# Attention and two bilinear layers on one core: v windows of 96 rows instead of 128, and a new order of the opening

## The chip, the cores and the metric

The kernel runs on one core of a Trainium2 chip. The metric is the device time of one execution in microseconds (us). The engines are named as in the profile: PE (TensorE matmuls; PEld its weight loads), DVE (VectorE), ACT (ScalarE), POOL (GpSimd) and SP (SyncE, which here issues every DMA).

## What is computed

The reference, cut to what matters (batch 2, 8 heads, 768 positions, head size 64; 1536 tokens of width 512):

```python
k_sum = k.reshape(B, H, nb, 32, D).max(axis=3)
v_sum = v.reshape(B, H, nb, 32, D).mean(axis=3)
scores_l = where(abs(i - j) < 16, scale * q @ k.T, -1e9)
scores_s = scale * q @ k_sum.T + log(32)
a = softmax(concat([scores_l, scores_s]))
x = a @ concat([v, v_sum])              # 1536 x 512 after the heads are put side by side
h = x @ w_in                            # d_ff 2048
x = (h * tanh(softplus(h))) @ w_out     # the first layer ("mish")
out = ((x @ w_a) * (x @ w_b)) @ w_out2  # the second, d_ff 1536
```

## The kernel before

**Attention.** Queries are cut into units of 64 (`U`). A unit sees 96 keys (`WK` = 64 + 2 x 16) and the 24 block sums, 120 columns in all (`SW`). Four units are a group g; there are six groups, three of each batch, and four pairs of heads p in each. For a pair, `batch_s` (L567, L571) makes the scores on PE, DVE adds the mask and finds the row's extreme with a custom instruction (L588, one per unit and head side; below "score pass"), ACT takes the exponential (L594), DVE sums, inverts and multiplies (L597, L599, L601, the last below "weight product"). `batch_o` transposes the weights on PE (L626), copies them out of PSUM (L377 on ACT or L378 on DVE), and multiplies by v (L638; for group 0 the sums' part apart, L651). The result x is kept as a rounded high part (CAST, L377/L378) and a low part (L668).

**Where v lies.** `load_windows` brings for each of the four units its window of v with the unit's first row in partition 0. Rows 96 to 119 of the same tile take the block means of v, which `prep_v` makes on PE (L492), `keep_v` copies out and `spread_v` copies by a DMA from SBUF to SBUF (`attn<-attn`). The block maxima of k are DVE reductions (L462). The windows of before are 128 partitions high, so that the spread must follow them.

**The layers.** `step1` does the first layer on the tokens that are ready, four slices of 128 columns of d_ff: L897 is x @ w_in, L927 the mish on ACT, L930 its low part, L944 the product with w_out. Weights come as 64-bit numbers; `convert` makes 32-bit ones of them (ACT L688, DVE L693 and L696) and `split` the high (ACT L377) and low (DVE L708) parts. After the attention follow the other slices of the first layer (L1076, L1121) and the second one (L1076, L1229), both on PE without a pause.

**What sets the order.** Every step is handed to a planner (`Plan`) with a due time and a cost on each engine that may do it. `emit` runs the plan through a list schedule (ready steps, earliest key first) and writes each engine's instructions in that order; on the chip each engine then keeps the order and waits by semaphores. Due times hang on `T0` (start of the first layer), `bt`/`out_t` (scores and output of a group) and `pace`. DMA durations, the extra key for a switch of ACT's function table (`TABLE_PENALTY`) or of PE's tile shape (`SHAPE_PENALTY`) are constants of the planner. Where PE would stand idle before `fill_end`, a matmul on a zero tile is put in, whose result nobody reads (`fill`, L434); eight of them also open the program:

```python
if pick is None and e == "PE" and ham_end > 3.5 and t < self.fill_end:
    ...
    pick = (t, e, "fill", fb[-1])
...
pl.fill, pl.fill_end = fill, T0 + -7.99
```

Of the kernel before, what the change touches and what calls it, by code (L numbers as in the profile page):

```python
# [34 lines left out]
class Plan:  # L35
# [8 lines left out]
    SAME, PE_SHAPE = 0.02, 0.095  # L44
    SHAPE_PENALTY = 1.6
    PINNED = -50.0
    DMA_LEAD, DMA_TAIL, DMA_RAMP = 0.62, 2.18, 8.0
    BACKLOG, DMA_SLACK, DMA_RING = 4.0, 0.5, 8
    TABLE, TABLE_PENALTY = 1.3, 5.37
    WARM, PAGE, PE_LEAD, FETCH, FETCH_BUSY = 0.34, 256, 64, (6.4, 2.6), 46.0  # L50
# [38 lines left out]
    def emit(self):  # L89
# [18 lines left out]
        ready = {e: [] for e in engines}  # L108
        free_at = {e: 0.0 for e in engines}
        bank_free, where, held = {b: 0.0 for b in range(8)}, {}, set()  # L110
# [12 lines left out]
        while done < n:  # L123
# [94 lines left out]
            if delay:  # L218
                dma_free = max(dma_free, end + self.DMA_LEAD) + delay * (1.35 if 2.0 < dma_free < self.DMA_RAMP else 1.0)
                end = dma_free + self.DMA_TAIL  # L220
                landed.append(end)
# [19 lines left out]
def attention_mish_moe_bilinear_moe(  # L241
# [23 lines left out]
    U = 64  # L265
# [7 lines left out]
    NEG = -1.0e9  # L273
    T0 = 20.47
    BITS64 = w_in.dtype != F32
# [484 lines left out]
    size = lambda b: GT * len(gran2[b])  # L760
    w_dma = {("in", 0): -88.93, ("out", 0): -85.34, ("in", 1): -93.01}
    pace = (6.36, 5.0, 6.2, 6.0, 5.4)
    att_in = {0: 4, 1: 8, 2: 8}
# [10 lines left out]

    D1 = 15.29
    seqL, tl = [], t
# [27 lines left out]

    SIGN = (T0 + 32.36, tl + 20.0)

    batches = [(g, p) for g in range(B * NG) for p in range(NP)]
    bt, out_t = {}, {}
    BG, SP = (26.14, 40, 48, 59.27, 73.73), (0.5, 1.0, 1.0, 1.08, 1.43)
    for g, p in batches:  # L810
        if g == 0:
            bt[g, p] = 5.46 + 1.76 * p
        else:
            bt[g, p] = BG[g - 1] + SP[g - 1] * p
        out_t[g, p] = bt[g, p] + (7.82 if g else 11.69)

    eps = 1.0e-3
    first_use = {}
    for vi, b, c, ts, dt in steps1:
        for kind, d in (("in", 0.0), ("out", 1.22 * dt)):  # L820
            first_use.setdefault((kind, c), ts + d)
# [10 lines left out]
    for b in range(B):  # L832
        g0 = NG * b
        if b == 0:
            pieces = [(T_S[0], 2), (T_S[2], 2)]
            kv, kd, ev = 9.86, -92.86, 1.5
        else:
            pieces = [(T_S[0], 2), (Y1, 2)]
            kv, kd = bt[g0, 0] - 3.2, bt[g0, 0] - 13.1
            ev = end_o(g0 - 2) + eps  # L840
        at_time(ev, lambda kv=kv, kd=kd, b=b, x=pieces: prep_v(kv, kd, b, x))
        at_time(ev, lambda kv=kv, b=b: keep_v(kv + 0.5, b))
        for p in range(NP):
# [499 lines left out]
```

## Time and profile before

| what | value |
|---|---|
| median of 3 runs | 595.54 us (595.42 to 596.45) |
| the profiled execution's own time | 595.54 us |
| its span, first to last instruction | 593.8 us |
| PE busy | 586.6 us (99%) |
| DVE, ACT busy | 489.2 us (82%), 318.8 us (54%) |
| mean granted TensorE clock | 0.996 |

1.74 us of the profiled execution lie outside its span. The shares are of the whole span: the attention, the first 100 us or so, is another stage than the 490 us after it, and is to be read by its own stretches.

### The profile page before, as it was taken

What the parts mean: (1) busy time and instruction counts of PE and PEld (TensorE: products, weight loads), DVE (VectorE), ACT (ScalarE), POOL (GpSimd) and SP (SyncE); (2) the same over time, 40 slices, a digit from 0 to 9 for tenths busy, and PEclk for the clock granted to TensorE, in tenths of its full rate; (3) what the DMA queues carried; (4) which work ended last, traced back from release to release, by engine and by line L of the source; (5) the groups of instructions that cost most, each with busy time, mean ns of one, the idle gap of its engine ahead of it and who ended that gap; (6) DMA issues with size and microseconds to landing.
All of it is one profiled execution on the core that took longest, in us unless ns stands there. A gap on an engine that the chain in (4) does not pass through costs nothing.

```text
span 593.8 us, 10770 instructions
## 1 busy us (share of the span) xinstructions
PE 586.6 (99%) x4162; PEld 530.9 (89%) x4163; DVE 489.2 (82%) x1134; ACT 318.8 (54%) x711; POOL 6.7 (1%) x34
## 2 busy tenths in 40 slices
PE   9999999999999999999999999999999999999998
PEld 5788788889898899989999999999898999999896
DVE  6899999999999988979799998858686876855443
ACT  5699999457555555455376655444262434433030
POOL 3000000000000000000000000000000000000000
PEclk9899999999999999999999999999999999999999
DMA  9997700222233221222003133230122212300202
GB/s 282 348 345 221 224 20 3 71 72 72 71 107 106 73 71 72 72 71 72 0 1 100 43 107 111 103 107 20 52 72 71 108 35 72 107 0 2 89 18 107
DMA packets 22288, 54.89 MB, mean 92 GB/s; under 512 B 1917, under 2 KB 8061, under 8 KB 22237
## 3 DMA queue, kind: packets, MB, share of 16 engines
q1 hardware_dynamic: 22236, 54.21, 27.8%
q8 instruction: 32, 0.52, 0.4%
q14 instruction: 20, 0.16, 0.1%
HBM read 50.07 MB, written 3.15 MB: 90 GB/s over the span
## 4 chain that ended last, share of the span: by engine, by line
PE 92%; ACT 3%; DVE 3%; DMA 1%; issue 1%; ACTq 0%
PE bank L1076 44%; PE bank L1121 17%; PE bank L1229 17%; PE bank L944 5%; PE bank L897 4%; ACT attn L594 2%; PE bank L567 1%; PE bank L638 1%; DMA attn<-attn 1%; PE bank L626 1%; PE bank L434 1%; DVE attn L588 1%; ACT L927 1%; ACT rounded L377 0%; PE bank L571 0%
## 5 line engine op out<-in xcount | busy, mean ns | idle before, releaser
L1076 PE MATMUL bank<-rounded,wext 128*128 128x384 f32 x1176 | 213.8, 335 | 0.0
L1076 PEld LDWEIGHTS bank<-rounded,wext 128*128 128x128 f32 x1176 | 205.7, 188 | 3.5
L377 ACT CAST rounded<-arena 128x384 fp32r<-128x384 f32 (+2 forms) x145 | 80.8, 568 | 88.9 <-PE bank L1229 37.4
L1121 PE MATMUL bank<-rounded,wext 128*128 128x512 f32 (+1 forms) x456 | 104.7, 380 | 0.0
L1229 PE MATMUL bank<-wext,rounded 128*128 128x512 f32 (+2 forms) x441 | 100.0, 386 | 0.0
L1089 DVE TENSOR_TENSOR arena<-arena,bank 128x384 f32<-128x384 f32 x132 | 71.8, 550 | 31.2 <-PE bank L1076 23.1
L1229 PEld LDWEIGHTS bank<-wext,rounded 128*128 128x128 f32 x441 | 82.0, 188 | 16.3
L1121 PEld LDWEIGHTS bank<-rounded,wext 128*128 128x128 f32 x456 | 83.9, 188 | 12.6
L1085 ACT COPY arena<-bank 128x384 f32<-128x384 f32 x108 | 51.5, 478 | 56.5 <-PE bank L1076 53.8
L377 ACT CAST wext<-arena 128x512 fp32r<-128x512 f32 (+1 forms) x80 | 49.0, 621 | 33.2 <-PE bank L1076 12.7
L1076 PE MATMUL bank<-rounded 128*128 128x384 f32 x336 | 61.1, 335 | 0.0
L1076 PEld LDWEIGHTS bank<-rounded 128*128 128x128 f32 x336 | 58.5, 188 | 0.2
L1125 DVE TENSOR_TENSOR arena<-bank,arena 128x512 f32<-128x512 f32 (+1 forms) x76 | 49.9, 658 | 10.0 <-PE bank L1121 9.9
L1248 DVE TENSOR_TENSOR arena<-bank,arena 128x512 f32<-128x512 f32 (+2 forms) x37 | 25.0, 677 | 34.5 <-PE bank L1229 34.5
L708 DVE TENSOR_TENSOR wext<-arena,wext 128x512 fp32r<-128x512 f32 (+1 forms) x80 | 49.8, 639 | 0.7 <-ACT wext L377 0.3
L696 DVE SCALAR_TENSOR_TENSOR arena<-arena 128x512 uint32<-128x512 uint32 x68 | 46.6, 689 | 2.3 <-ACT arena L688 0.4
L708 DVE TENSOR_TENSOR rounded<-arena,rounded 128x384 fp32r<-128x384 f32 (+2 forms) x72 | 40.9, 583 | 4.8 <-ACT rounded L377 4.3
L594 ACT ACTIVATE attn<-attn 128x120 f32<-128x120 f32 x96 | 36.7, 386 | 7.6 <-DVE attn L588 7.5
L944 PE MATMUL bank<-rounded 128*128 128x512 f32 (+1 forms) x168 | 37.1, 367 | 0.0
L688 ACT ACTIVATE arena<-arena 128x512 f32<-128x512 f32 x38 | 25.8, 680 | 17.7 <-DMA arena<-in_w_out_dram 9.4
L897 PE MATMUL bank<-rounded 128*128 128x512 f32 (+1 forms) x168 | 35.3, 363 | 0.0
L897 PEld LDWEIGHTS bank<-rounded 128*128 128x128 f32 x168 | 28.1, 189 | 4.7
(75 smaller groups left out, 546.3 us busy)
## 6 DMA issues: line engine op xcount, KB each, us to landing
arena<-in_w_out_dram SPq DMA_DIRECT2D x28, 512.0 KB, 3.3
arena<-in_w_in_dram SPq DMA_DIRECT2D x16, 512.0 KB, 3.9
arena<-in_w_a_dram SPq DMA_DIRECT2D x12, 512.0 KB, 4.1
arena<-in_w_b_dram SPq DMA_DIRECT2D x12, 512.0 KB, 3.3
arena<-in_kT_dram SPq DMA_DIRECT2D x8, 384.0 KB, 9.6
out_dram<-arena SPq DMA_DIRECT2D x11, 256.0 KB, 2.0
attn<-in_qT_dram SPq DMA_DIRECT2D x5, 512.0 KB, 8.7
attn<-in_v_dram SPq DMA_DIRECT2D x3, 768.0 KB, 7.3
```

Source lines behind the costliest of these rows:

```text
L377: alts = [("ACT", act_us(n), lambda env: nc.scalar.copy(out=dst(env), in_=src(env))), ("DVE", dve2_us(n) if fast else dve_us(n), lambda en ...
L594: act(key, SW + 90, lambda env, x=x: nc.scalar.activation(out=s[:, x, :], in_=s[:, x, :], func=AF.Exp, scale=-1.0, bias=negm[:, x:x + 1], ...
L696: dve(key, 512, lambda env: nc.vector.scalar_tensor_tensor(out=f.bitcast(U32), in0=hw.bitcast(U32), scalar=3, in1=f.bitcast(U32), op0=ALU. ...
L708: dve(key, n, lambda env: nc.vector.tensor_sub(out=r32(lo[0]()), in0=src, in1=hi[0]()), r=rd + hi[1], w=lo[1])
L897: nc.tensor.matmul(like(dst, b), lt, rt, start=(j == 0), stop=(j == 3 * KC - 1))
L944: nc.tensor.matmul(yp, lt, r32(rt), start=(fst and j == 0), stop=(lst and j == 2))
L1076: nc.tensor.matmul(dst, lt, r32(rt), start=(start and i == 0 and j == 0), stop=(last and i == 1 and j == 2), skip_group_check=True)
L1085: act(k, TN, lambda env: nc.scalar.copy(out=dst[0], in_=bank[env[nm[z]]][:, 0:TN]), w=[nm[z]] + dst[1])
L1089: dve(k, TN, lambda env: op(out=dst[0], in0=dst[0], in1=bank[env[nm[z]]][:, 0:TN]), w=dst[1] + [nm[z]], free=[nm[z]] if free else [])
L1121: nc.tensor.matmul(dst, lt, rt, start=(q == 0), stop=(q == 5))
L1125: dve(k + 1.2, n, lambda env: nc.vector.tensor_add(acc, bank[env[yn]][:, 0:n].rearrange(*shape[2], **shape[3]), acc), w=[yn] + ak, free=[yn])
L1229: nc.tensor.matmul(dst, lt, rt, start=(opens and j == 0), stop=(closes and j == n_mm - 1))
```

## The change

The window loads end at partition 96 (`WK`) instead of 128, and the one that starts at the sequence's edge at 80 rows instead of 112. The spread of the block means writes rows 96 to 119, so it is no longer tied to the windows. Beside it the planner's constants change: a start of 0.8 us for each engine, other durations for the first DMAs (`RAMP`), a dearer switch of ACT's table (5.37 to 19.03) and of PE's shape, and fillers allowed up to `T0` + 3.64; and some twenty due times of the opening. Nothing is computed differently.

```diff
-    SHAPE_PENALTY = 1.6
+    SHAPE_PENALTY = 2.39
-    DMA_LEAD, DMA_TAIL, DMA_RAMP = 0.62, 2.18, 8.0
+    DMA_LEAD, DMA_TAIL, DMA_RAMP = 0.62, 1.57, 8.0
+    START, RAMP = 0.8, ((2.8, 1.0), (7.3, 1.75), (11.0, 1.0), (1.0e9, 0.95))
-    TABLE, TABLE_PENALTY = 1.3, 5.37
+    TABLE, TABLE_PENALTY = 1.3, 19.03
...
-    pl.fill, pl.fill_end = fill, T0 + -7.99
+    pl.fill, pl.fill_end = fill, T0 + 3.64
...
         dma(key, ar(vw_o[vs], GU, HD)[WK:SW, :, :], src, r=[("vm", p) for p in range(NP)],
-            w=[("vw", vs, j, h) for j in range(3) for h in range(2)] + [("vsum", vs)], nbytes=NB * GU * HD * 4)
+            w=[("vsum", vs)], nbytes=NB * GU * HD * 4)
...
-            dma(key, t[WIN:P, 0, :], v[b, 0:P - WIN, :], w=both(0), nbytes=(P - WIN) * HD * 4)
+            dma(key, t[WIN:WK, 0, :], v[b, 0:WK - WIN, :], w=both(0), nbytes=(WK - WIN) * HD * 4)
...
-            src = bass.AP(base.tensor, base.offset + h, [[HD, P], [U * HD, u1 - u0], [1, m]])
-            dma(key + 0.0001 * h, t[:, u0:u1, h:h + m], src, w=[("vw", s, 1, h // m)] if m < HD else both(1),
-                nbytes=(u1 - u0) * P * m * 4)
+            src = bass.AP(base.tensor, base.offset + h, [[HD, WK], [U * HD, u1 - u0], [1, m]])
+            dma(key + 0.0001 * h, t[0:WK, u0:u1, h:h + m], src, w=[("vw", s, 1, h // m)] if m < HD else both(1),
+                nbytes=(u1 - u0) * WK * m * 4)
...
-    BG, SP = (26.14, 40, 48, 59.27, 73.73), (0.5, 1.0, 1.0, 1.08, 1.43)
+    BG, SP = (26.14, 39.55, 48, 59.27, 73.73), (0.27, 1.0, 1.0, 0.61, 1.21)
```

One line is added near the top, so every line below stands one further down in the new kernel (L588 becomes L589).

**SP, the loads behind the first four k and q tiles** (`in_v` into `attn` is a window, into `arena` the raw v for the block means; `attn<-attn` is the spread). Before:

```order
L364 DMA attn<-in_v_dram 112x512
L364 DMA attn<-in_v_dram 128x3x256 x2
L364 DMA arena<-in_w_in_dram 128x1024
L364 DMA arena<-in_v_dram 128x2x256 x4
L364 DMA arena<-in_w_in_dram 128x1024
L364 DMA attn<-in_qT_dram 128x4x256
L364 DMA attn<-in_v_dram 128x4x256 x2
L364 DMA arena<-in_w_out_dram 128x1024
L364 DMA attn<-in_qT_dram 128x4x256
```

Of the change:

```order
L365 DMA attn<-in_v_dram 80x512
L365 DMA attn<-in_v_dram 96x3x256 x2
L365 DMA arena<-in_v_dram 128x2x256 x4
L365 DMA arena<-in_w_in_dram 128x1024 x2
L365 DMA attn<-in_qT_dram 128x4x256
L365 DMA arena<-in_w_out_dram 128x1024
L365 DMA attn<-in_v_dram 96x4x256 x2
L365 DMA attn<-attn 24x4x512
L365 DMA attn<-in_qT_dram 128x4x256
```

Raw v now goes ahead of the first w_in, the first w_out ahead of group 1's windows, and group 1's spread stands ahead of group 2's q (it came four issues behind it).

**DVE, from its first reduction of k** (L588/L589 ISA is a score pass, of bank 62/63 for pair 0; the reads of its result are left out). Before:

```order
L462 TENSOR_REDUCE attn<-arena 128x24
L588 ISA attn<-bank_62,attn 128x120
...
L588 ISA attn<-bank_63,attn 128x120
...
L462 TENSOR_REDUCE attn<-arena 128x24
L588 ISA attn<-bank_62,attn 128x120
```

Of the change:

```order
L463 TENSOR_REDUCE attn<-arena 128x24
L589 ISA attn<-bank_62,attn 128x120
...
L463 TENSOR_REDUCE attn<-arena 128x24
L589 ISA attn<-bank_63,attn 128x120
...
L589 ISA attn<-bank_62,attn 128x120
...
L589 ISA attn<-bank_63,attn 128x120
L589 ISA attn 128x1
L598 TENSOR_SCALAR attn<-attn 128x4
L600 RECIPROCAL attn<-attn 128x4
L463 TENSOR_REDUCE attn<-arena 128x24
```

Pair 1's reduction comes one score pass earlier, and pair 0's sums (L598) stand ahead of pair 2's reduction; before, they stood behind it.

**ACT, the exponentials of group 1 and the first mish** (L594/L595 exponential, L927/L928 mish, L688/L689 and the CAST into `rounded` weight conversion). Before:

```order
L594 ACTIVATE attn<-attn 128x120 x7
L688 ACTIVATE arena<-arena 128x512
L594 ACTIVATE attn<-attn 128x120 x3
L377 CAST rounded<-arena 128x512
L594 ACTIVATE attn<-attn 128x120 x6
L927 ACT_TABLE_LOAD
L927 ACTIVATE arena<-bank_68 128x256
```

Of the change:

```order
L689 ACTIVATE arena<-arena 128x512
L378 CAST rounded<-arena 128x512
L595 ACTIVATE attn<-attn 128x120 x16
L928 ACT_TABLE_LOAD
L928 ACTIVATE arena<-bank_64 128x256
```

The conversion that stood among the sixteen exponentials is now done ahead of them.

## Rows read from the trace of the kernel before

**Rows 1.** The page, busy time: engine, us, share, instructions.

```profile
PE 586.6 (99%) x4162; PEld 530.9 (89%) x4163; DVE 489.2 (82%) x1134; ACT 318.8 (54%) x711; POOL 6.7 (1%) x34
```

**Rows 2.** Busy time by stretches: stretch, length, each engine's busy us, clock, DMA share, GB/s.

```profile
26.00:35.00 9.00, 7.43 (x137) 6.69 (x137) 8.57 (x38) 8.95 (x32) 0.00 (x0) 1.00 1.05 300
...
45.00:55.00 10.00, 9.61 (x188) 8.47 (x187) 9.94 (x32) 9.94 (x28) 0.00 (x0) 1.00 0.90 260
...
66.00:80.00 14.00, 14.00 (x203) 11.62 (x195) 13.69 (x55) 13.90 (x37) 0.52 (x1) 1.00 0.46 137
```

**Rows 3.** What PE waited for: us in total, times, longest.

```profile
PE bank L626 <- DVE attn L601: 1.6, 3, 0.6
```

**Rows 4.** PE in order of time: start us, us, instruction, count, [idle before <- releaser].

```profile
5.79 1.68 PE L434 MATMUL bank<-attn 128*128 128x512 bf16 x7
...
25.84 3.17 PE L897 MATMUL bank<-rounded 128*128 128x256 f32 x24
...
34.59 0.62 PE L626 MATMUL bank<-attn 128*120 128x128 f32 x4 [0.65 <-DVE attn L601]
...
54.14 0.65 PE L626 MATMUL bank<-attn 128*120 128x128 f32 x4 [0.39 <-ACT arena L927]
...
64.53 1.15 PE L638 MATMUL bank<-attn 120*64 120x64 f32 x32 [0.53 <-DMA attn<-attn]
```

**Rows 5.** DVE in order of time, same columns.

```profile
6.04 0.28 DVE L588 CUSTOM_DVE_ANT_0 attn<-bank,attn 128x120 f32<-128x120 f32 x1 [0.93 <-POOL attn L415]
...
6.63 0.95 DVE L462 TENSOR_REDUCE attn<-arena 128x24 f32<-128x768 f32 x1
...
16.57 0.65 DVE L601 TENSOR_TENSOR attn<-attn 128x480 f32<-128x480 f32 x1
...
19.53 0.61 DVE L378 COPY attn<-bank 24x128 f32<-24x128 f32 x2 [1.11 <-ACT attn L377]
...
24.16 0.27 DVE L588 CUSTOM_DVE_ANT_0 attn<-bank,attn 128x120 f32<-128x120 f32 x1
...
33.80 0.65 DVE L601 TENSOR_TENSOR attn<-attn 128x480 f32<-128x480 f32 x1
```

**Rows 6.** Chain of waits, pieces on DVE: start us, us, line, count.

```profile
10.74 0.87 DVE attn L462
...
12.14 0.57 DVE attn L601
12.71 1.22 DVE attn L588 x12
...
15.53 0.33 DVE arena L693
...
15.96 0.71 DVE arena L696
```

**Rows 7.** ACT in order of time.

```profile
24.54 0.40 ACT L594 ACTIVATE attn<-attn 128x120 f32<-128x120 f32 x1 [1.70 <-DVE attn L588]
...
26.83 0.38 ACT L594 ACTIVATE attn<-attn 128x120 f32<-128x120 f32 x1
...
31.39 0.38 ACT L594 ACTIVATE attn<-attn 128x120 f32<-128x120 f32 x1
...
31.88 1.28 ACT L927 ACT_TABLE_LOAD   x1
```

**Rows 8.** TensorE's clock by stretches, columns as in rows 2.

```profile
22.00:22.50 0.50, 0.50 (x33) 0.44 (x25) 0.50 (x2) 0.50 (x2) 0.00 (x0) 1.00 1.05 371
22.50:23.00 0.50, 0.50 (x18) 0.50 (x19) 0.50 (x3) 0.34 (x2) 0.00 (x0) 0.51 1.06 383
...
26.00:26.50 0.50, 0.50 (x5) 0.50 (x6) 0.50 (x6) 0.50 (x5) 0.00 (x0) 1.00 0.98 381
```

**Rows 9.** SP's DMA issues in order of time.

```profile
57.50 0.38 SPq L364 DMA_DIRECT2D attn<-in_qT_dram  x1
58.44 0.82 SPq L364 DMA_DIRECT2D attn<-attn  x1
```

More of the change, by code (lines that the diff above doesn't have):

```diff
@@ L108, in emit @@
         ready = {e: [] for e in engines}
-        free_at = {e: 0.0 for e in engines}
+        free_at = {e: self.START for e in engines}
         bank_free, where, held = {b: 0.0 for b in range(8)}, {}, set()
@@ L218, in emit @@
             if delay:
-                dma_free = max(dma_free, end + self.DMA_LEAD) + delay * (1.35 if 2.0 < dma_free < self.DMA_RAMP else 1.0)
+                dma_free = max(dma_free, end + self.DMA_LEAD) + delay * next(f for lim, f in self.RAMP if dma_free < lim)
                 end = dma_free + self.DMA_TAIL
@@ L273, in attention_mish_moe_bilinear_moe @@
     NEG = -1.0e9
-    T0 = 20.47
+    T0 = 20.27
     BITS64 = w_in.dtype != F32
@@ L760, in attention_mish_moe_bilinear_moe @@
     size = lambda b: GT * len(gran2[b])
-    w_dma = {("in", 0): -88.93, ("out", 0): -85.34, ("in", 1): -93.01}
-    pace = (6.36, 5.0, 6.2, 6.0, 5.4)
+    w_dma = {("in", 0): -91.19, ("out", 0): -85.34, ("in", 1): -91.79}
+    pace = (6.36, 5.0, 6.11, 5.49, 5.4)
     att_in = {0: 4, 1: 8, 2: 8}
@@ L773, in attention_mish_moe_bilinear_moe @@
     slot_of = {kc: EW[i] for i, kc in enumerate((k, c) for c in range(NG1) for k in ("in", "out"))}
-    D1 = 15.29
+    D1 = 15.46
     seqL, tl = [], t
@@ L803, in signed_at @@
         return key < SIGN[0] or key > SIGN[1]
-    SIGN = (T0 + 32.36, tl + 20.0)
+    SIGN = (T0 + 36.55, tl + 20.0)
     batches = [(g, p) for g in range(B * NG) for p in range(NP)]
     bt, out_t = {}, {}
-    BG, SP = (26.14, 40, 48, 59.27, 73.73), (0.5, 1.0, 1.0, 1.08, 1.43)
+    BG, SP = (26.14, 39.55, 48, 59.27, 73.73), (0.27, 1.0, 1.0, 0.61, 1.21)
     for g, p in batches:
         if g == 0:
-            bt[g, p] = 5.46 + 1.76 * p
+            bt[g, p] = 4.98 + 1.76 * p
         else:
             bt[g, p] = BG[g - 1] + SP[g - 1] * p
-        out_t[g, p] = bt[g, p] + (7.82 if g else 11.69)
+        out_t[g, p] = bt[g, p] + (4.9 if g else 11.62)
     eps = 1.0e-3
@@ L819, in attention_mish_moe_bilinear_moe @@
     for vi, b, c, ts, dt in steps1:
-        for kind, d in (("in", 0.0), ("out", 1.22 * dt)):
+        for kind, d in (("in", 0.0), ("out", 0.89 * dt)):
             first_use.setdefault((kind, c), ts + d)
@@ L835, in attention_mish_moe_bilinear_moe @@
             pieces = [(T_S[0], 2), (T_S[2], 2)]
-            kv, kd, ev = 9.86, -92.86, 1.5
+            kv, kd, ev = 10.44, -93.21, 1.5
         else:
             pieces = [(T_S[0], 2), (Y1, 2)]
-            kv, kd = bt[g0, 0] - 3.2, bt[g0, 0] - 13.1
+            kv, kd = bt[g0, 0] - 2.76, bt[g0, 0] - 12.65
             ev = end_o(g0 - 2) + eps
@@ L843, in attention_mish_moe_bilinear_moe @@
         for p in range(NP):
-            kk, kd = (bt[g0, p] - 4.19, -100.0 + p) if b == 0 else (bt[g0, p] - 3.0, bt[g0, 0] - 6.96 + 0.5 * p)
+            kk, kd = (bt[g0, p] - 4.14, -100.0 + p) if b == 0 else (bt[g0, p] - 3.0, bt[g0, 0] - 5.78 + 0.5 * p)
             ev = end_s(g0 - 1) if b else 1.0
@@ L848, in attention_mish_moe_bilinear_moe @@
     for g in range(B * NG):
-        kq, kw = [(-99.5, -94.0), (-85.86, -85.4)][g] if g < 2 else (bt[g, 0] - 0.92, bt[g, 0] - 4.68)
+        kq, kw = [(-99.5, -94.0), (-85.72, -82.79)][g] if g < 2 else (bt[g, 0] - -0.94, bt[g, 0] - 1.47)
         at_time(end_s(g - 2) if g >= 2 else 1.0, lambda k=kq, g=g: load_q(k, g))
@@ L868, in need @@
         if (kind, c) not in w_at:
-            load_w(first_use[kind, c] - 7.48, kind, c, slot_of[kind, c])
+            load_w(first_use[kind, c] - 4.62, kind, c, slot_of[kind, c])
     def cut(offs, n, i=0):
@@ L1257, in expand @@
                 keep()
-    combine_x1(A_, t - 18.9)
-    combine_x1(B_, t - 1.27)
+    combine_x1(A_, t - 14.25)
+    combine_x1(B_, t - 3.23)
     done_l = set()
```

## The prediction

> **What bounds the kernel now.** I read the busy times first: PE is busy 586.6 of 593.8 us [rows 1], so what can be won is small. It is PE's idle time, its fillers and the stretch at the lower clock; the useful matmuls are the same in both kernels. Then I asked where PE stands: the busy times by stretches show 14.00 of 14.00 us from 66 us on, but 7.43 of 9.00 between 26 and 35 us, while ACT has 8.95 and DVE 8.57 there [rows 2]. So the opening, up to about 65 us, is bound by DVE and ACT by turns, and from then on PE runs without a gap: a microsecond that PE comes earlier to 65 us is a microsecond off the end, and one that DVE or ACT saves counts only if PE comes earlier by it. The list of PE's waits names where: 1.6 us of its idle time are three waits for weight products [rows 3]. In order of time the last of these ends at 34.59 us; one of 0.39 us for a mish ends at 54.14 and one of 0.53 us for a spread at 64.53 [rows 4]. These three moments are the posts at which I measure the change.
>
> **The bytes.** Of 24 window units 22 lose 32 rows of 2 KB: 22 x 64 KB = 1.44 MB, 0.26 MB of it in each of the first two groups. At the 371 GB/s of [rows 8] that is 0.7 us a group. No PE wait in [rows 3, 4] is for a window, so I put the bytes themselves at nothing: the DVE and ACT chains cover them. What they could cost, if that cover went, is at most those 0.7 us, and what they may give is the same.
>
> **Fillers: nothing.** The change has 20 of them instead of 26 (8, 3, 4, 1, 4 where there were 8, 7, 6, 2, 3), each some 0.24 us (1.68 us for seven [rows 4]). They fill waits for DVE and loads; with fewer, PE stands idle in their place. [...]
>
> **Up to 17 us: nothing, between -0.4 and +0.9.** DVE leads here. Its prices: reduction 0.87, weight product 0.57, a score pass 0.20 (six of them with their reads in 1.22) [rows 6]; an exponential 0.38 ((26.83 - 24.54) / 6 [rows 7]). The first pass starts at 6.04, released by POOL, and pair 1's reduction at 6.63, some 0.1 us after the second pass is through [rows 5], so I take it that k landed about then. In the new order this reduction goes ahead of pass two: passes two to four run from 7.50 to 8.10, their exponentials, from 7.8 on, end at about 9.1, and only then come the sums that now stand ahead of pair 2's reduction. DVE idles for about 1 us. Against that, pair 1's scores are ready some 0.4 us earlier, and the first steps of the weight conversion (0.33 + 0.71 [rows 6]) no longer stands ahead of pair 3's weight product. Walked through to the last product of group 0 I get 16.7 us where it is 16.57 [rows 5]: no gain. The idle microsecond alone would be +0.9, the earlier scores alone -0.4.
>
> **17 to 24 us: nothing.** The new order does three conversions before group 1's score passes where there were two (0.33 + 0.71 more on DVE, and a split), and one copy of weights out of PSUM fewer. DVE has a hole of 1.11 us before 19.53 [rows 5] that takes what is left. By the walk the passes begin at 24.15; they began at 24.16.
>
> **24 to 35 us: -1.2 us.** With the third conversion done, the sixteen exponentials stand in one row: from about 24.5, 16 x 0.38 = 6.1 us, they end at 30.6, where the last began at 31.39 and the table load came at 31.88 [rows 7]. It then comes at about 30.7, and the first mish 1.2 us earlier than now. On DVE the conversion's steps (0.33 + 0.71 and the split) leave this stretch as well, and a first step (0.33) stays: the fourth weight product comes at 32.6 instead of 33.80 [rows 5]. So PE's transposes of pair 3 start at 33.3 to 33.4 instead of 34.59 [rows 4]. Bounds: nothing, if a step ahead of the passes is late by as much; -2.0, if PE leads: its 24 matmuls of L897 end at 29.0 (25.84 + 3.17 [rows 4]), and with x ready at 23.3, as I walk it, they would end at about 27 at the upper clock (24 x 0.13 us, and half of the scores between them). I take -1.2, since in my walk PE waits for DVE twice in this stretch, whatever its clock does.
>
> **35 to 65 us: -0.5 us.** The whole program has 11 table loads instead of 15, at 1.28 us each [rows 7], two of the four saved before 55 us, in the stretch where ACT is busy 9.94 of 10.00 us [rows 2]. The mish on which the transposes wait 0.39 us [rows 4] now comes in the same table visit as the two before it. So this wait should go; late next is DVE, busy 9.94 us too, whose last weight product of group 2 I walk to 53.4, that is, only 0.75 us ahead of the 54.14. The last post is the spread of group 3: it was issued at 58.44, 0.9 us behind 512 KB of q issued at 57.50 [rows 9], and PE waited 0.53 us for it. In the new order this q stands behind the spread. But three of its four source copies stand on ACT behind eight exponentials, and I walk the issue to 57.3: 1.1 us earlier, plus up to 1.4 us (512 KB at 371 GB/s) for the q that is out of the way. Of the 0.92 us of the two waits I count half: between nothing at all, and all of them.
>
> **After 65 us: nothing.** PE runs through. The number of places where PE's instruction changes its kind is 251 instead of 249, and the useful matmuls are equal in number.
>
> **Sum.** The profiled execution took 595.54 us, which is the median too; -1.2 and -0.5 give 593.8 us. With -0.4 to +0.9, 0 to -2.0 and 0 to -0.9 as the ends of the terms, this case's own range is 592.9 to 594.9.
>
> **The rivals.**
>
> *More is won (0.20).* TensorE keeps its upper clock and DVE and ACT come early enough to let PE use it. Now the granted clock falls to 0.51 at 22.5 us and is back at 26 [rows 8]: 3.4 us at half of the speed, 1.7 us of work. The new order puts twelve dense L898 matmuls between the halves of group 1's scores. PE would then be through with L898 at about 27, 2.0 us earlier, and with both later waits gone (0.92) the time is 592.6. Against it: the x that these matmuls need is ready at 23.3 by my walk, after the fall.
>
> *The wait moves on (0.23): about 595.0.* Two places. The spread of group 1 stands ahead of group 2's q and waits for the copies of the means, which end at 18.5 in my walk: with the spread's own 0.8 us [rows 9] that q leaves SP at 19.4 or later, behind its present place. And the last product of group 2, or the spread of group 3, stays where it was, since DVE is as busy as ACT [rows 2]. Then most of the 1.2 us is given back before 65 us, and the result lies within 0.2% (1.2 us) of no change, about what a measurement can tell.
>
> *Slower (0.11): about 597.0.* [...]
>
> [...]
>
> **How the numbers follow.** The likeliest case has 0.46: 593.8 us. Its upper quarter and a little lies within 0.2% of the old time. Faster by over 0.2% (below 594.35): 0.20 from the first rival, 0.38 of the 0.46, a little of the second: 0.60. Within 0.2%: 0.29. Slower by more: 0.11. The range takes in the first rival to half a microsecond below its time and the second wholly, and leaves out the slower one: 591.9 to 596.2.
>
> **What would show it.** Right: group 1's exponentials in one row ending near 30.6 us, the last transposes of group 1 near 33.3, no PE wait for a mish near 54, PE without a gap from about 64 on, 11 table loads. Wrong: score passes of group 1 that begin later than 24.5; a clock below 1 before 21.6; PE waiting for q at the scores of group 2; or a wait of over 1 us for the spread near 63 us.

## The result, and the profile of the changed kernel

The changed kernel takes **603.1 us** (median of 6 runs, 600.99 to 604.23), the kernel before 595.57 (6 runs, 595.42 to 596.45): a ratio of **1.0119, 95% interval 1.0098 to 1.014**. The forecast was 593.8, with a range up to 596.2. The sign was wrong, and the range did not hold the time. One execution of run 10 below (723.38 us) and one of the kernel before beside runs 5 to 7 (626.31) ran at a lower mean clock (0.751 and 0.943) and are left out of what follows. The profiled execution of the changed kernel took 604.23 us, 8.7 more than that of before.

In the changed kernel the helper lines stand one lower: its L627 is L626 of before, its L898 is L897, and so on. The page's busy time and DMA queue 1 (packets, MB, share of the 16 engines' span):

```profile
PE 588.7 (98%) x4157; PEld 532.5 (88%) x4157; DVE 484.7 (80%) x1120; ACT 319.3 (53%) x721; POOL 6.7 (1%) x34
q1 hardware_dynamic: 21308, 52.76, 27.9%
```

From 66 us on PE waits for nothing in either kernel; DVE and ACT are busy about as long as in [rows 1]. The queue moves 1.45 MB less than before (54.21 MB there) and still takes 27.9% of the engines' time, in a longer span. Busy time by stretches, with the columns of [rows 2]:

```profile
20.00:25.00 5.00, 5.00 (x109) 4.04 (x106) 4.94 (x12) 3.85 (x8) 0.52 (x1) 0.74 1.11 232
22.00:22.50 0.50, 0.50 (x10) 0.12 (x10) 0.50 (x2) 0.10 (x1) 0.10 (x1) 0.85 1.11 229
...
26.00:35.00 9.00, 7.12 (x188) 6.39 (x186) 6.92 (x44) 8.70 (x36) 0.00 (x0) 1.00 1.06 297
35.00:40.00 5.00, 2.47 (x20) 2.29 (x20) 3.89 (x11) 3.03 (x4) 0.00 (x0) 1.00 1.04 271
45.00:55.00 10.00, 6.91 (x62) 6.14 (x64) 7.20 (x33) 7.63 (x26) 0.00 (x0) 0.90 1.03 266
53.50:60.00 6.50, 6.23 (x136) 5.68 (x140) 6.11 (x21) 5.37 (x16) 0.00 (x0) 0.51 0.34 119
66.00:80.00 14.00, 14.00 (x279) 12.03 (x271) 13.76 (x59) 13.56 (x40) 0.52 (x1) 1.00 0.81 207
```

The same view of the kernel before, for the two stretches that [rows 2] do not have:

```profile
20.00:25.00 5.00, 5.00 (x122) 4.09 (x126) 4.49 (x18) 2.99 (x9) 0.43 (x1) 0.75 1.07 364
35.00:40.00 5.00, 5.00 (x119) 4.76 (x118) 5.00 (x20) 4.99 (x16) 0.52 (x1) 1.00 1.04 377
```

The last two columns are the news. In both kernels the transfer engines are busy all the time in these two stretches (1.04 to 1.11), but from 20 to 25 us they move 232 GB/s instead of 364, and from 35 to 40 us 271 instead of 377. Between 35 and 40 us PE, DVE and ACT all have holes that they did not have before. ACT (1.36 us, until 36.16) and DVE (3.10 us, until 36.11, below) wait there for w_out, and PE for DVE. PE's waits between 4 and 80 us (us in total, times, longest):

```profile
PE bank L493 <- DMA attn<-in_v_dram: 3.1, 1, 3.1
PE bank L627 <- DVE attn L600: 2.9, 1, 2.9
PE bank L627 <- ACT attn L595: 1.3, 1, 1.3
PE bank L572 <- DVE attn L463: 0.8, 1, 0.8
```

All rows of this view add up to 9.1 us; in the kernel before they add up to 3.1, of which [rows 3] are 1.6. That is 6.0 us. The longest of them ends at 53.77 us. Right behind it, from 53.5 to 60 us the granted clock is 0.51, where it was 1.00 from 26 to 40 us: 6.5 x 0.49 = 3.2 us of work not done. The stretch at the lower clock that [rows 8] show is there in both kernels (0.74 and 0.75 from 20 to 25 us). 6.0 + 3.2 = 9.2, against the 8.7 us by which the two profiled executions differ.

PE, DVE and ACT in order of time, to be read beside [rows 4], [rows 5] and [rows 7]:

```profile
24.67 2.17 PE L898 MATMUL bank<-rounded 128*128 128x256 f32 x12
...
31.42 0.62 PE L627 MATMUL bank<-attn 128*120 128x128 f32 x4 [1.26 <-ACT attn L595]
37.33 0.62 PE L627 MATMUL bank<-attn 128*120 128x128 f32 x4 [2.95 <-DVE attn L600]
38.16 0.63 PE L627 MATMUL bank<-attn 128*120 128x128 f32 x4 [0.21 <-ACT arena L689]
...
53.77 1.92 PE L493 MATMUL bank<-attn 80*24 80x128 f32 x32 [3.09 <-DMA attn<-in_v_dram]
```

```profile
16.61 0.66 DVE L602 TENSOR_TENSOR attn<-attn 128x480 f32<-128x480 f32 x1
18.50 0.43 DVE L694 TENSOR_SCALAR arena<-arena 128x512 uint32<-128x512 uint32 x1 [1.23 <-DMA arena<-in_w_in_dram]
...
25.95 0.28 DVE L589 CUSTOM_DVE_ANT_0 attn<-bank,attn 128x120 f32<-128x120 f32 x1
...
36.11 0.43 DVE L694 TENSOR_SCALAR arena<-arena 128x512 uint32<-128x512 uint32 x1 [3.10 <-DMA arena<-in_w_out_dram]
36.52 0.65 DVE L602 TENSOR_TENSOR attn<-attn 128x480 f32<-128x480 f32 x1
37.36 0.65 DVE L602 TENSOR_TENSOR attn<-attn 128x480 f32<-128x480 f32 x1
```

```profile
26.63 0.40 ACT L595 ACTIVATE attn<-attn 128x120 f32<-128x120 f32 x1
...
32.35 0.38 ACT L595 ACTIVATE attn<-attn 128x120 f32<-128x120 f32 x1
...
32.84 1.28 ACT L928 ACT_TABLE_LOAD   x1
```

Up to 16.6 us, the last weight product of group 0, nothing is lost. Then DVE waits 1.23 us for the first weights w_in, the score passes of group 1 begin at 25.95 instead of 24.16, and at 36.11 a conversion step that waits 3.10 us for w_out stands ahead of the last two weight products of the group. They come at 36.52 and 37.36, where the forecast had the last of them at 32.6; PE's wait of 2.95 us for the first of them is put down by the profile to the small step beside it (L600). Until 53.77 us PE waits 3.09 us for the windows of group 3.

### The profile page after: what moved, and what is told of

Same layout as the page of the kernel before. It is cut to its first block, busy times and chain, and to the rows that moved or that the text cites. A ratio compares the mean times of both kernels' runs of the same rounds, so it can differ in the third digit from the quotient of the medians.

```text
span 602.5 us, 10741 instructions
## 1 busy us (share of the span) xinstructions
PE 588.7 (98%) x4157; PEld 532.5 (88%) x4157; DVE 484.7 (80%) x1120; ACT 319.3 (53%) x721; POOL 6.7 (1%) x34
## 3 DMA queue, kind: packets, MB, share of 16 engines
q1 hardware_dynamic: 21308, 52.76, 27.9%
## 4 chain that ended last, share of the span: by engine, by line
PE 85%; DMA 7%; DVE 6%; ACT 1%; issue 1%; SPq 1%; DVEq 0%; ACTq 0%
PE bank L1077 39%; PE bank L1230 16%; PE bank L1122 14%; PE bank L945 5%; PE bank L898 4%; DMA arena<-in_w_out_dram 3%; DMA attn<-in_v_dram 2%; PE bank L639 2%; DMA arena<-in_w_in_dram 1%; DVE rounded L999 1%; PE bank L568 1%; PE bank L627 1%; DMA attn<-in_qT_dram 1%; DVE arena L1002 1%; DVE rounded L709 1%
## 5 line engine op out<-in xcount | busy, mean ns | idle before, releaser
L378 ACT CAST rounded<-arena 128x384 fp32r<-128x384 f32 (+3 forms) x151 | 83.0, 565 | 95.7 <-PE bank L1230 41.5
L1077 PEld LDWEIGHTS bank<-rounded 128*128 128x128 f32 x336 | 58.4, 188 | 1.1 <-DVE arena L1090 0.9
L709 DVE TENSOR_TENSOR rounded<-arena,rounded 128x384 fp32r<-128x384 f32 (+1 forms) x72 | 40.8, 581 | 2.5 <-ACT rounded L378 1.9
L595 ACT ACTIVATE attn<-attn 128x120 f32<-128x120 f32 x96 | 36.7, 387 | 7.8 <-DVE attn L589 7.6
L689 ACT ACTIVATE arena<-arena 128x512 f32<-128x512 f32 x38 | 25.8, 681 | 19.8 <-DMA arena<-in_w_b_dram 8.0
L898 PE MATMUL bank<-rounded 128*128 128x512 f32 (+1 forms) x168 | 35.5, 365 | 0.0
L1164 ACT ACTIVATE arena<-arena 128x384 f32<-128x384 f32 x36 | 18.9, 526 | 27.5 <-DVE arena L1090 27.5
```

The lines of the kernel that those rows point to most:

```text
L378: alts = [("ACT", act_us(n), lambda env: nc.scalar.copy(out=dst(env), in_=src(env))), ("DVE", dve2_us(n) if fast else dve_us(n), lambda en ...
L595: act(key, SW + 90, lambda env, x=x: nc.scalar.activation(out=s[:, x, :], in_=s[:, x, :], func=AF.Exp, scale=-1.0, bias=negm[:, x:x + 1], ...
L709: dve(key, n, lambda env: nc.vector.tensor_sub(out=r32(lo[0]()), in0=src, in1=hi[0]()), r=rd + hi[1], w=lo[1])
L898: nc.tensor.matmul(like(dst, b), lt, rt, start=(j == 0), stop=(j == 3 * KC - 1))
L1077: nc.tensor.matmul(dst, lt, r32(rt), start=(start and i == 0 and j == 0), stop=(last and i == 1 and j == 2), skip_group_check=True)
```

## The experiments

All times are medians, beside the kernel before on the same chip (595.6 to 595.9 us). The change has two halves, the shape of the loads and the plan, and the first two runs take them apart.

**1. The 96 rows alone.** The order on every engine is that of before.

```diff
...
-            src = bass.AP(base.tensor, base.offset + h, [[HD, P], [U * HD, u1 - u0], [1, m]])
+            src = bass.AP(base.tensor, base.offset + h, [[HD, WK], [U * HD, u1 - u0], [1, m]])
...
```

> The kernel before with its order untouched on every engine; only the window loads end at partition 96 (80 rows instead of 112 at the sequence's edge). Theory 1 (the shape: a load to 96, 80 or 112 partitions moves fewer bytes per us than one to 128, the DMA engines are full anyway, and everything queued behind comes late): 598 to 605 us, the rate falls to some 200 to 250 GB/s while the window loads of groups 0 and 1 run, and DVE or ACT waits for weights. Theory 2 (the order: raw v ahead of w_in, the spread ahead of group 2's q, fewer fillers): 594.8 to 595.7 us, since the order is the old one and the bytes are 1.44 MB fewer.

Measured: **599.69 us**, ratio 1.0068 (1.0054 to 1.0083). Fewer bytes, nothing else, and 3.8 us slower, as theory 1 had it. In the profiled execution, PE in order of time shows a wait with no releaser in the middle of the scores of group 1:

```profile
23.03 0.27 PE L567 MATMUL bank<-arena,attn 64*64 64x96 f32 x1
26.05 0.43 PE L567 MATMUL bank<-arena,attn 64*64 64x96 f32 x4 [2.75 <-issue]
```

**2. The new plan alone, with loads of 128 rows.** The changed kernel, with the rows of before.

```diff
...
-            src = bass.AP(base.tensor, base.offset + h, [[HD, WK], [U * HD, u1 - u0], [1, m]])
+            src = bass.AP(base.tensor, base.offset + h, [[HD, P], [U * HD, u1 - u0], [1, m]])
...
```

> The change with its new planner constants, but window loads of 128 rows as before, with the spread behind them again; the first sixteen issues on SP come in the changed kernel's order. Theory 1 (the shape): 592.5 to 595.5 us, about the 593.8 of the prediction, since the walk along DVE and ACT held and only the loads were late. Theory 2 (the order): 600 to 604 us, as the changed kernel.

Measured: **600.0 us**, 1.0073 (1.0061 to 1.0085): 4.1 us slower, as theory 2 had it. So each theory holds for its half, and each half costs about 4 us, 3.8 + 4.1 = 7.9, where the change as a whole costs 7.5. DVE in order of time has the wait for w_in and the late passes without any short load. But the conversion step that waits 3.10 us for w_out in the changed kernel (the fourth L694) does not wait here, nor does PE wait for a window. Both waits are missing in run 1 too, so neither half alone shows them: the two halves nearly add up in time, but they do not lose it at the places where the whole change does:

```profile
18.68 0.43 DVE L694 TENSOR_SCALAR arena<-arena 128x512 uint32<-128x512 uint32 x1 [1.84 <-DMA arena<-in_w_in_dram]
...
26.25 0.28 DVE L589 CUSTOM_DVE_ANT_0 attn<-bank,attn 128x120 f32<-128x120 f32 x1
...
32.28 0.42 DVE L694 TENSOR_SCALAR arena<-arena 128x512 uint32<-128x512 uint32 x1
```

**3. Each load of 96 rows as 64 and 32**, in the changed kernel.

```diff
-        pl.add(key, [("SP", 0.48, lambda env: nc.sync.dma_start(out=dst, in_=src))],
...
+            nc.sync.dma_start(out=dst[0:U], in_=src[0])
+            nc.sync.dma_start(out=dst[U:WK], in_=src[1])
...
```

> The changed kernel with its own order; each window load of 96 rows is issued as two, partitions 0 to 63 and 64 to 95, which costs SP some 0.4 us an issue for ten more issues. The loads of 80 rows stay. Theory 1 (the shape): if loads of 64 and 32 partitions run at the rate of 128, 593 to 597 us; if they are as slow as 96 in one piece, 600 to 604. Theory 2 (the order): 600 to 604 us.

Measured: 604.49 us, 1.016 (1.0126 to 1.0194), no better than the changed kernel. Cutting the load does not mend it.

**4. The loads by themselves.** This kernel computes nothing, and its output is zeros: it loads windows of v into four buffers, four loads of four units for each shape, and DVE copies columns of each when it has landed. It was executed once, as was run 8.

```diff
+    def window(t, rows, p0=0, c0=0, cols=HD):
...
+        src = bass.AP(base.tensor, base.offset + c0, [[HD, rows], [U * HD, 4], [1, cols]])
+        nc.sync.dma_start(out=t[p0:p0 + rows, :, c0:c0 + cols], in_=src)
```

> Window loads alone, nothing else of the kernel (the output is zeros): ten phases of four windows each, one after the other, of 128, 112, 96, 80 and 64 rows, 96 rows as 64 and 32, 128 and 96 rows in half columns, then 128 and 96 again. Theory 1 (the shape): 128 rows at 330 to 400 GB/s, 96 rows at 250 or less, so that a phase of 96 rows takes as long as one of 128 or longer. Theory 2 (the order): the same GB/s within a tenth for 128 and 96 rows, a phase of 96 rows three quarters as long.

DVE in order of time; from one start to the next is the time of a load when they follow each other. The first two lines are of 128 rows (1 MiB), the next two of 96 (768 KB), the next two of 64 (512 KB). In the last four each window was loaded in two halves of 256 columns, and a line stands for the second half: two lines of 128 rows, two of 96:

```profile
12.97 0.15 DVE L32 COPY got<-win 128x1 f32<-128x1 f32 x1 [2.92 <-DMA win<-in_v_dram]
15.65 0.15 DVE L32 COPY got<-win 128x1 f32<-128x1 f32 x1 [2.46 <-DMA win<-in_v_dram]
...
38.37 0.15 DVE L32 COPY got<-win 128x1 f32<-128x1 f32 x1 [3.22 <-DMA win<-in_v_dram]
41.61 0.15 DVE L32 COPY got<-win 128x1 f32<-128x1 f32 x1 [3.02 <-DMA win<-in_v_dram]
...
66.40 0.15 DVE L32 COPY got<-win 128x1 f32<-128x1 f32 x1 [2.40 <-DMA win<-in_v_dram]
69.01 0.15 DVE L32 COPY got<-win 128x1 f32<-128x1 f32 x1 [2.40 <-DMA win<-in_v_dram]
...
91.48 0.15 DVE L32 COPY got<-win 128x1 f32<-128x1 f32 x1 [1.28 <-DMA win<-in_v_dram]
...
94.49 0.15 DVE L32 COPY got<-win 128x1 f32<-128x1 f32 x1 [1.29 <-DMA win<-in_v_dram]
...
104.66 0.15 DVE L32 COPY got<-win 128x1 f32<-128x1 f32 x1 [1.44 <-DMA win<-in_v_dram]
...
107.79 0.15 DVE L32 COPY got<-win 128x1 f32<-128x1 f32 x1 [1.35 <-DMA win<-in_v_dram]
```

A load of 128 rows takes 2.68 us, one of 96 rows **3.24 us**: three quarters of the bytes in 1.2 times the time, 243 GB/s instead of 391. 112 rows took 3.98 us, 80 rows 3.00, 64 rows 2.61, and 64 followed by 32 rows 3.5. So by itself the shorter load holds the transfer engines longer (their busy share in the phase of 96 rows is 1.06, at 236 GB/s, from 38 to 45 us). In halves, the form in which the kernel loads the windows of its first two groups, the gap is small: 3.0 us for 128 rows and 3.1 to 3.2 for 96.

**5. The new plan with the old order of the first loads**, 128 rows.

```diff
-    w_dma = {("in", 0): -91.19, ("out", 0): -85.34, ("in", 1): -91.79}
+    w_dma = {("in", 0): -88.93, ("out", 0): -85.34, ("in", 1): -93.01}
-            kv, kd, ev = 10.44, -93.21, 1.5
+            kv, kd, ev = 10.44, -92.86, 1.5
...
```

> The run with 128 rows and the new planner constants, but the first loads in the old order: one w_in ahead of raw v, group 1's windows ahead of the first w_out. Theory A (the order's 4 us come from the loads: w_in behind raw v makes DVE stand 1.8 us at its first weight step, ahead of the copies of the means and of group 1's score passes): passes of group 1 begin at 24.0 to 24.6 us instead of 26.25, and the time is 593.5 to 596. Theory B (the rest of the plan: table penalty, due times, filler limits): the passes may be earlier, but the time stays at 598 to 601.

Measured: 599.91 us, 1.0063 (1.0051 to 1.0075). The wait for w_in went and the passes of group 1 began at 24.16, as before, but the 4 us stayed: theory B. PE's waits between 15 and 60 us:

```profile
PE bank L627 <- DVE attn L602: 2.1, 2, 1.3
PE bank L572 <- issue: 1.9, 1, 1.9
```

**6. The other way round: before, with only the new order of the first loads.**

```diff
-    w_dma = {("in", 0): -88.93, ("out", 0): -85.34, ("in", 1): -93.01}
+    w_dma = {("in", 0): -91.19, ("out", 0): -85.34, ("in", 1): -91.79}
-            kv, kd, ev = 9.86, -92.86, 1.5
+            kv, kd, ev = 9.86, -93.21, 1.5
-        kq, kw = [(-99.5, -94.0), (-85.86, -85.4)][g] if g < 2 else ...
+        kq, kw = [(-99.5, -94.0), (-85.72, -82.79)][g] if g < 2 else ...
```

> The kernel before, 128 rows and all of its constants, with the new order of the first loads alone (raw v ahead of both w_in, the first w_out ahead of group 1's windows); its planner plans the rest around it. Theory A (the loads): 597.5 to 600.5 us, DVE waits 1 to 2 us for w_in at its first weight step. Theory B (the rest of the plan): 595 to 596.5 us.

Measured: 599.82 us, 1.0067 (1.0055 to 1.0079). The time is that of theory A, its sign is not: DVE does not wait for w_in here, though the passes of group 1 begin late, at 25.23. So the order of the first loads alone costs 3.9 us, the rest of the plan alone 4.0, and both together 4.1: the two do not add up.

**7. Before, with only the higher penalty for a change of ACT's table.**

```diff
-    TABLE, TABLE_PENALTY = 1.3, 5.37
+    TABLE, TABLE_PENALTY = 1.3, 19.03
```

> The kernel before with the dearer switch of ACT's table alone (5.37 to 19.03): 11 table loads instead of 15. Theory A (the loads): 594.5 to 596 us, the loads are the old ones and ACT is freed of 5.1 us. Theory B (the rest of the plan): 597 to 600 us, since holding the mish back until the exponentials are through makes the first layer's products late and leaves PE without work between 30 and 40 us.

Measured: **595.59 us** (11 runs) beside 595.9, ratio 0.9990 (0.9981 to 0.9998), with 11 table loads instead of 15. This part does no harm, and of all kernels run it is the only one not slower than the kernel before; the gain is below the 0.2% that a measurement here can tell. Four loads of 1.28 us fewer bring 0.3 us at most, so nearly all of their 5.1 us must have lain beside other work.

**8. More row counts, loads alone** (computes nothing, output zeros): run 4 with other counts.

```diff
+    for rows in (128, 120, 104, 96, 72, 48, 32, 16, 128):
+        for t in bufs:
+            window(t, rows)
```

> Window loads alone again (the output is zeros): phases of four windows of 128, 120, 104, 96, 72, 48, 32, 16 and again 128 rows. If what counts is that the partitions split evenly over 16 engines in whole groups of eight, 120 and 104 rows (neither a multiple of 16) are slowest, at 150 GB/s or less, 96 near 240 as before, 48 and 32 below 200. If a load costs the same whatever its rows (as 64 rows took as long as 128), every phase takes 2.6 to 4 us a load and the rate falls in proportion to the rows.

Measured between landings: 128 rows 2.69 us, 120 rows 4.6, 104 rows 4.6, 96 rows 3.2, 72 rows 3.2 to 4.6, 32 rows 1.3 to 1.45, and 2.73 for 128 rows at the end. 120 and 104 rows take longest, as expected, but at 213 and 187 GB/s and not at 150 or less. Every count tried from 120 down to 72 takes longer than the full 128.

**9 and 10. Where the 96 rows cost.** Before, with 96 rows from the third group on, and its counterpart with 96 rows in the first two groups. Up to here I had a second theory: that run 1 lost its time by the one wait with no releaser, which I took for PE's own instructions coming late.

```diff
...
+        R = WK if g >= 2 else P
-            src = bass.AP(base.tensor, base.offset + h, [[HD, P], [U * HD, u1 - u0], [1, m]])
+            src = bass.AP(base.tensor, base.offset + h, [[HD, R], [U * HD, u1 - u0], [1, m]])
...
```

In run 10 the first line reads `R = WK if g < 2 else P`.

> The order of before on every engine; only the windows from the third group of units on are loaded with 96 rows, the first two groups keep 128. Theory A (each load of 96 rows holds the transfer engines longer, and the sum of it counts): the six later groups carry most of the bytes, so most of the 3.8 us that 96 rows cost with the old order shows again, 598 us or more. Theory F (what cost the time in the run with 96 rows throughout is one late supply of instructions to PE at 23 to 26 us, 2.7 us of standing in the scores of the second group, and the 3.4 us at half clock behind it): the first two groups are as before, so no wait of over 0.5 us with no visible releaser in the scores of the second group, and 595 to 596.5 us.

> The counterpart: 96 rows in the first two groups alone, 128 rows later. Theory A (the sum of the longer loads): a small part of the 3.8 us, 595.5 to 597. Theory F (one late supply of instructions at 23 to 26 us): the whole of it, 598.5 to 600.5 us, with PE standing 1.5 to 3 us with no visible releaser in the scores of the second group, and in the trace an instruction packet that comes 2 us or more later than the one at 19.9 us of before.

Measured: 598.07 us (1.004, 1.0025 to 1.0055) for the later groups (there are four of them, not six) and 597.08 (1.0023, 1.001 to 1.0036) for the first two, at the upper edge of what theory A gave. 2.2 + 1.2 = 3.4, within the intervals of the 3.8 us of run 1. Both times lie outside what theory F gave, so the loss stands in both parts and not in one place: as an account of run 1, theory F fell. Its wait of 2.7 us is in neither trace, though the profiled execution of run 10 took only 596.23 us and so shows little of the loss. Theory A holds in kind and not in size. An estimate from run 4: the 13 full units of the later groups are 0.14 us each longer, 1.8 us in all, and the 7 of the first two groups, loaded in halves, 0.05 each, 0.3 us, where 2.2 and 1.2 us were lost.

**11. Only PE's instructions moved.** Before, with every filler written as two halves.

```diff
-        nc.tensor.matmul(bank[b], warm[:, 0:P], warm, start=True, stop=True)
+        for c in (0, 256):
+            nc.tensor.matmul(bank[b][:, c:c + 256], warm[:, 0:P], warm[:, c:c + 256], start=True, stop=True)
```

> The kernel before with every filler matmul of 512 columns of the opening written as two of 256: the same columns on PE, 26 matmuls and 26 weight loads more before the first 13 us, nothing else moved, all loads as before. Theory F (PE's instructions come in pages of 256; in every run so far the waits with no visible releaser stand at PE instructions 705, 1217 and 1729, multiples of 256 apart, and end 1.4 us after an instruction packet has landed): the edges of the pages fall 52 instructions earlier in the order; the page from 21.9 to 26.8 us of before is then done in 4.9 us, where a page takes 6.3 us or more to come while the transfers are full, so PE stands 1 to 3 us with no visible releaser at about 26 to 28 us (at PE instruction 961), and the kernel takes 596.5 to 599 us. Theory A (only transfers and their waits decide): within 0.5 us of before.

Measured: **597.12 us**, 1.0023 (1.001 to 1.0035). PE in order of time; the count of PE's matmuls and weight loads up to the wait (the windows view, 474 and 475); and DMA queue 8 in the 1.2 us from 24.6 us on:

```profile
24.08 0.98 PE L898 MATMUL bank<-rounded 128*128 128x256 f32 x6
27.06 2.31 PE L898 MATMUL bank<-rounded 128*128 128x256 f32 x18 [2.01 <-issue]
```

```profile
0.00:25.50 25.50, 23.54 (x474) 18.17 (x475) 18.55 (x77) 14.32 (x49) 5.65 (x32) 1.00 0.97 320
```

```profile
q8 instruction: 1, 0.02, 5.8%
```

The same count for run 1, up to its wait:

```profile
0.00:23.10 23.10, 21.16 (x347) 12.94 (x347) 15.40 (x60) 12.84 (x43) 5.68 (x32) 1.00 0.97 287
```

The wait came where it was foretold: 949 against 694 by these counts, 255 later (961 and 705 in the expectation, which counted otherwise). In run 5 the count at the wait is 1202, in run 3 it is 1702. In runs 1, 5 and 11 an instruction packet (1.1 us) ends 1.3 to 1.5 us ahead of the end of the wait. So I read such a wait, in which no engine and no load is named, as PE standing for its own instructions; the view counts their packet on the same 16 transfer engines as the loads (5.8% of the 1.2 us above). As an effect theory F holds: 26 matmuls and as many weight loads more in idle time cost 1.2 us. The planner of both kernels has pages of instructions among its constants (`PAGE` 256, `FETCH` 6.4 us for one up to 46 us and 2.6 after), and in the kernel before PE's waits with no engine and no load named add up to only 0.2 us between 4 and 80 us: its order was planned around the edges.

**12. The changed kernel, with the later windows due as early as before.**

```diff
-        ... (bt[g, 0] - -0.94, bt[g, 0] - 1.47)
+        ... (bt[g, 0] - -0.94, bt[g, 0] - 4.68)
```

> The changed kernel with one number put back: the due time of the windows from the third group on (4.68 us ahead of their use, as before, in place of 1.47). PE's order is that of the changed kernel; on SP the windows of the fourth group stand ahead of one load of raw v and one of w_out. Theory: the wait of 3.1 us for v's windows at 50 to 54 us and the 6.8 us at half clock behind it, about 3.4 us of loss, go for the most part: 597.5 to 600.5 us, and the granted clock stays 1.00 from 50 to 60 us. Rival (the wait only changes its place, because the transfers are full until then and something else is late in the windows' stead): 601.5 to 604 us.

Measured: 602.28 us, 1.0106 (1.0088 to 1.0124). The rival holds. PE's waits between 4 and 80 us:

```profile
PE bank L627 <- DVE attn L602: 4.0, 1, 4.0
PE bank L493 <- DMA attn<-in_v_dram: 2.1, 1, 2.1
```

The wait for the windows lost 1.0 us and the one for the weight product, which itself waits behind w_out, gained 1.1. Here a load put forward made another late.

**13. Run 5 with 11 fillers halved.** The edit of run 11, for the first 11 fillers alone.

```diff
...
+        split = len(halved) < 11
+        halved.append(b)
+        for c in (0, 256) if split else (0,):
+            n = 256 if split else 512
-        nc.tensor.matmul(bank[b], warm[:, 0:P], warm, start=True, stop=True)
+            nc.tensor.matmul(bank[b][:, c:c + n], warm[:, 0:P], warm[:, c:c + n], start=True, stop=True)
```

> The kernel with the new plan, loads of 128 rows and the old order of the first loads (599.91 us), with the first 11 filler matmuls of 512 columns written as two of 256: 22 instructions more on PE before the first 13 us, nothing else moved. Theory F (a good part of that kernel's 4 us is PE's standing for its instructions in the scores of the third group, 1.9 us at PE instruction 1217): the edge of the page now falls 22 instructions earlier in the order; worked out from that run's own times with 6.4 us for a page to come, the wait falls from 2.1 to 0.5 us, and nothing of over 0.6 us stands in its place: 597.5 to 599 us. Rival (that wait only takes the place of others, by q, the spread or DVE, which are late anyway): 599.3 us or more, with the wait's 1.9 us seen again in waits for DVE, ACT or a transfer between 28 and 45 us.

Measured: 600.55 us, 1.0077 (1.0064 to 1.009): a miss. PE in order of time:

```profile
37.78 0.40 PE L574 MATMUL bank<-arena,attn 64*64 64x96 f32 x8 [2.26 <-issue]
51.31 1.07 PE L499 MATMUL bank<-attn 80*24 80x128 f32 x32 [1.84 <-DMA attn<-in_v_dram]
```

The edge moved 11 matmuls and 11 weight loads forward, as meant, but PE went on 9.8 us after the edge before it (28.0 us) instead of 6.3 (31.2 in run 5), so the wait did not shrink, and one for v followed. With the transfers as full in both runs (share 1.04 to 1.07 from 20 to 40 us), a page did not take the same time in the two.

**14. Before, with only the planner's costs of the change.** Due times, rows and the order of the first loads are the old ones.

```diff
-    DMA_LEAD, DMA_TAIL, DMA_RAMP = 0.62, 2.18, 8.0
+    DMA_LEAD, DMA_TAIL, DMA_RAMP = 0.62, 1.57, 8.0
+    START, RAMP = 0.8, ((2.8, 1.0), (7.3, 1.75), (11.0, 1.0), (1.0e9, 0.95))
...
```

> The kernel before with only the planner's costs of the change (the ramp of the transfers, their tail, the start, the penalties for a change of shape and of table); every due time, the order of the first loads and the 128 rows are as before. Theory (the plan was fitted to one set of costs, and what costs 4 us in the kernel with the new plan and the old loads is any other order in the crowded stretch up to 60 us, not a certain due time): 597 to 600.5 us. Rival (the due times make the loss, the costs are as harmless as the table penalty was alone at 595.59): 595 to 596.5 us.

Measured: **600.89 us**, 1.0087 (1.0068 to 1.0107). PE's waits between 4 and 80 us:

```profile
PE bank L639 <- issue: 2.1, 1, 2.1
PE bank L627 <- ACT attn L595: 1.9, 1, 1.9
PE bank L572 <- DVE attn L463: 1.4, 3, 0.8
PE bank L568 <- issue: 1.1, 1, 1.1
```

No due time is needed for the loss, nor the new order of the first loads. Runs 2, 5, 6 and 14 are four different orders, and all lie at 599.8 to 600.9 us. Their profiled executions, beside that of before, by two views: the sum of PE's waits between 4 and 80 us, and what the lower clock took (span x (1 - mean granted clock), which is known to some 0.3 us), both as differences from before (3.1 us, and 593.8 x 0.004 = 2.4 us). The executions of the four runs lie 3.1 to 7.1 us above that of before, where the medians lie 4 to 5 above, so a row tells of its execution and not of the median:

| run | PE's waits | lower clock | sum | span less 593.8 |
|---|---|---|---|---|
| 2, new plan | +4.0 | +1.2 | +5.2 | +5.9 |
| 5, new plan, old first loads | +2.5 | -0.6 | +1.9 | +3.1 |
| 6, new first loads | +0.8 | +3.0 | +3.8 | +4.1 |
| 14, new costs | +5.1 | +3.6 | +8.7 | +7.1 |
| the change | +6.0 | +2.4 | +8.4 | +8.7 |

The two columns account for the spans to within 1.6 us. The loss is made up differently each time. In run 6 most of it is the clock, which was at 0.51 from 30 to 40 us; in run 5 the clock costs less than before, and waits make it.

**What stays open.** No single wait explains the 4 us that a new order costs at 128 rows; shown is only that four orders lose it in waits and at the lower clock in four different mixtures, and that mending one wait (runs 5, 12 and 13) brought others. Why a load of 96 rows is slower than one of 128 is not shown either, only that it is, and the longer loads by themselves come to about 2 of the 3.8 us that they cost.

## Why the prediction was wrong, by its own steps

**The bytes: "at nothing, at most 0.7 us a group".** This step failed, in sign. I priced 32 rows at bytes over rate. A load of 96 rows runs at 243 GB/s where 128 rows run at 391, so a load of four units takes 0.56 us *more* (run 4; in halves 0.1 to 0.2), and the 96 rows alone cost 3.8 us (run 1), spread over early and late groups (runs 9, 10). The cover that I named, DVE and ACT, covers a window that comes late, but not what stands behind it in the queue: the transfer engines were full, the share was 1.05 to 1.06 in [rows 8], and I read only the GB/s. What came late in run 1 was PE's instructions, as I read its wait of 2.75 us. In the changed kernel it was w_out (3.10) and the windows of group 3 (3.09), for which neither run 1 nor run 2 waits: those two waits came only with the 96 rows and the new order together.

**17 to 24 us: "nothing".** Failed. I walked DVE's steps with w_in there when wanted. The plan issues the first w_in behind 1 MB of raw v, DVE waits 1.23 us for it, and the passes begin at 25.95 instead of 24.15. Run 2 has the same wait (1.84) with 128 rows and run 5, with the old order of loads, has none and passes at 24.16: this one was the order of the loads, not their shape. It is not the whole of what the order costs: run 5 loses its 4 us all the same, and of that half of the loss the cause stays open.

**24 to 35 us: -1.2 us.** The walk of ACT was right but for its start: sixteen exponentials in a row, 26.63 to 32.73, 6.1 us, the table load just behind them. The walk of DVE failed on one sentence, "a first step (0.33) stays": that step waits 3.10 us for w_out, and the weight products stand behind it in DVE's order, so PE's transposes came at 37.33 and 38.16 instead of 33.3. I had priced an instruction that waits for a load by its duration alone. The wait is no matter of the order alone: in run 2, with 128 rows, the same step waits for nothing.

**35 to 65 us: -0.5 us.** The two waits that I halved are gone, as foretold, and there are 11 table loads. In their place PE waits 3.1 us for the windows of group 3, and right behind it the clock is 0.51, from 53.5 to 60 us. The table loads are worth at most 0.3 us by themselves (run 7).

**Fillers, up to 17 us, after 65 us.** Right as far as seen: DVE idled for 0.90 us ahead of pair 0's sums, about the 1 us foretold, the last weight product of group 0 stood at 16.61 for the 16.7 foretold, and PE runs without a gap from 66 us on. No run changes the fillers' number alone, and what they do for the clock is not shown; it was 1.00 up to 22.3 us, with 20 fillers as with 26.

**The range.** The ends that the sum lists add up to 592.2 and 596.4 us, not to the 592.9 and 594.9 that it gives as its own range, and half a microsecond below the first rival's 592.6 is 592.1, not 591.9. No end of any of them reaches 603.1: a loss by the bytes had at most 0.7 us a group, and a loss by the order of the loads had no term in the sum.

**The rivals.** "The wait moves on" is what happened in kind, but I looked for it at q of group 2 and at the spread, where PE waits for neither (its one wait for a q, 0.4 us, stands in group 0), not at w_in, w_out and v. "Slower" was put at 597.0 by an estimate of mine, whose terms no run of the changed kernel shows: the clock was 1.00 up to 22.3 us, and the passes were late, at 25.95, behind the wait of 1.23 us for w_in. Of the signs that I named, passes later than 24.5 was the one that showed.

## What to carry to other kernels

Price a load by its measured time in its own shape, with the transfer engines' busy share beside it: here that share was 1.04 to 1.11, the load of fewer bytes was the longer one by 0.56 us (run 4), and what stood behind it came late, weights (3.10 us) and, as I read run 1, instructions (2.75 us) too. Where the transfers are full, check for each step put ahead of others on its engine which load it waits for; its price is that wait (here 3.10 us), not its duration (0.43). And change the shape and the order in separate runs first: here each alone already showed the loss.

## What the runs showed of the hardware that was not expected

The time of a load of four units against its rows is no line: 64 rows 2.61 us, 80 rows 3.00, 96 rows 3.24, 112 rows 3.98, 120 rows 4.6, and 128 rows 2.68 (runs 4 and 8). From 32 to 64 rows the time about doubles and the rate hardly changes: 256 KB in 1.3 to 1.45 us is 181 to 202 GB/s (run 8), 512 KB in 2.61 us is 201 (run 4).

PE's instructions stand among the loads as well: in the kernel before, the view of the DMA queues has 32 packets of queue 8 ("instruction") for PE's 8,325 matmuls and weight loads, one for about 260, and in run 4, which has no matmul, none of that queue. With the edges counted 256 instructions apart and the transfers full (share 1.04 to 1.10 in these stretches), PE went on 5.2 us (run 11), 6.3 (run 5), 9.8 (run 13) and 10.3 us (run 1) after the edge before. In run 5 it did the 256 instructions in 4.2 us, most of them the scores' many small matmuls, and stood for 1.9. In the kernel before, the packet for the scores of group 1 ends at 21.1 us, and PE reaches that edge at 22.5: no slack over the 1.3 to 1.5 us seen in the other runs, and no wait.
